# Agent attention with a cosine feed-forward: the exponentials sixteen steps later, GpSimd's row sums in wider sets

## The chip, the cores and the metric

The kernel runs on one core of one Trainium2 chip (trn2). The metric is the device time of one execution in microseconds (us); lower is better. The engines are named as the profile names them: PE is TensorE, PEld its weight loads, DVE is VectorE, ACT is ScalarE, POOL is GpSimd and SP issues the DMAs.

## What is computed

```
scale = 1 / sqrt(128)
def sm(a, b):
    s = scale * (a @ b.transpose(0, 2, 1))
    e = exp(s - s.max(-1))
    return e / (e.sum(-1) + 1e-9)
agent_v = sm(agents, k) @ v                # 4 batches, 49 agents, 12480 keys, 128 columns
x = sm(q, agents) @ agent_v                # 4 x 12480 rows, 128 columns
h = x @ w_in                               # 49920 rows, 2048 columns
out = (h * cos(h)) @ w_out                 # 49920 rows, 128 columns
```

## The kernel before

Nothing of `x` is stored. Since `x` is a product of 49 weights per query row with `agent_v`, the kernel multiplies `agent_v` into `w_in` once per batch (`project`, giving the tile `a`) and then needs, for each row, only the 49 weights. A **group** is 960 query rows (`GRP`); a batch has 13 of them. A **step** is one eighth of one half of a group: 16 steps to a group, 208 to a batch, 832 in all, and the loop at the end of the file runs over them.

In a step PE multiplies the group's turned weights `pT` with two slices of `a` (`first_product`, L1119), into a score buffer `ph` of which there are three; ACT takes the cosine (L1122); DVE forms `r = (cos - 1) * h` in one instruction (`cubic_part`, L1128); and four steps later PE multiplies `r` with `w_out` (`second_product`, L1144), whose missing linear part is added by two small products (L1140, L1141) at the end of each half group.

Everything else is done beside these steps, by a plan (`plan`, `extra`) that gives each piece of work a step number:

- *Keys*: for the next batch, 13 key groups are scored (L560), copied, and their running maximum is kept by POOL (L577 to L579); then the maximum over all is spread (`across`, `spread`) and POOL subtracts it (L604).
- *Queries*: each query group is scored (L169, L177 for some), copied, its row maximum taken (L734) and subtracted by POOL (L736, L782). Groups are gathered in **pieces** of up to seven: in each batch the eighth group up to the fourteenth, and the six behind them, which reach into the next batch. The first piece of a batch is first used at its step 128.
- *The burst*: cosine and exponential need different tables on ACT, so all exponentials of a batch are done together, at step 97 of the batch (`BURST`): the first piece of queries (L791), the keys (L607), the second piece (L791). During a burst DVE has no cosines to work on, so other work is put there (`fill`): three or four query groups of the next piece, two value groups, the test `judged`. There are four bursts, at steps 97, 305, 513 and 721. The last has no keys and no such filling.
- *Behind the burst*: POOL adds up each query row's 49 exponentials (`query_sum`, L802 to L806, a tree of additions over 24, 12, 6 and 3 columns, then three more) and, for a whole piece, adds EPS (L808); DVE takes the reciprocal of the whole piece (`query_inverse`, L814), 16 steps behind the burst for the first piece and 42 for the second. The groups of the first piece are summed at steps 1, 1, 3, 3, 9, 11 and 13 behind the burst.
- *Weights*: ten steps before a group's first step POOL multiplies its exponentials with the reciprocals (`query_weights`, L819), seven steps before it PE transposes the product (L833), ACT copies it (L838), and POOL casts it (L843) and takes what the cast lost (L844) into `pT`.
- *Values*: the 13 value groups of the next batch are multiplied with the keys' exponentials (L524) and added on DVE (L641); POOL adds the keys' exponentials (`add`, L613); then `agent_v` is folded and multiplied into `w_in` (L381).

Each engine runs its own queue in order. Where `kept_behind` or `as_traced` is used the order is as written; elsewhere a scheduler may move an instruction within its engine's queue. Around a burst PE, DVE and ACT are kept in the written order; POOL is not.

The plan of a burst, and the piece's closing addition, read:

```python
for i, n in zip((1, 1, 3, 3, 9, 11, 13), piece):
    plan(t + i, lazy_sum, n)
plan(t + (16, 42)[second], query_inverse, piece)
...
if n in closes:
    nc.gpsimd.tensor_scalar_add(rz_of[closes[n]], rz_of[closes[n]], EPS)
```

Of the kernel before, what the change touches and what calls it, by code (L numbers as in the profile page):

```python
# [9 lines left out]
F32 = mybir.dt.float32  # L10
# [8 lines left out]
P = 128  # L19
# [4 lines left out]
GT = 8  # L24
# [22 lines left out]
def agent_attention_cos_ffn(ctx, tc, qT, kT, v, vk, vk_rest, agT, w_in, w_out, outT):  # L47
# [625 lines left out]
    with ExitStack() as pools:  # L673
# [29 lines left out]
        NSTEP = NB * PER  # L703
        e_of, rz_of, closes = {}, {}, {}
        PIECES = 7

        def piece_tiles(piece):
            e = sb.tile([QT, PIECES * GT, NA], F32, name="e", bufs=3)
            rz = sb.tile([QT, PIECES * GT], F32, name="rz2", bufs=4)
            for i, k in enumerate(piece):  # L710
                e_of[k], rz_of[k] = e[:, i * GT:(i + 1) * GT], rz[:, i * GT:(i + 1) * GT]
                e_of[piece], rz_of[piece] = e[:, :len(piece) * GT], rz[:, :len(piece) * GT]
            if piece != early:
                closes[piece[-1]] = piece

# [79 lines left out]

        def query_sum(n):

            e, rz = e_of[n], rz_of[n].unsqueeze(2)
            t = sb.tile([e.shape[0], GT, 24], F32, name="tree", bufs=1)
            src, w = e, 24  # L800
            while w > 2:
                nc.gpsimd.tensor_add(t[:, :, :w], src[:, :, :w], src[:, :, w:2 * w])  # L802
                src, w = t, w // 2
            nc.gpsimd.tensor_add(rz, t[:, :, 0:1], t[:, :, 1:2])
            nc.gpsimd.tensor_add(rz, rz, t[:, :, 2:3])
            nc.gpsimd.tensor_add(rz, rz, e[:, :, 48:49])  # L806
            if n in closes:
                nc.gpsimd.tensor_scalar_add(rz_of[closes[n]], rz_of[closes[n]], EPS)  # L808

        def query_inverse(piece):  # L810
            rz = rz_of[piece]
            if piece not in closes.values():
                nc.vector.tensor_scalar_add(rz, rz, EPS)
            nc.vector.reciprocal(rz, rz)  # L814
# [43 lines left out]
        assert NG == 13  # L858
        BURST, LAST = 97, 97
        WINDOW = 7  # L860
# [96 lines left out]
        def summed(t, n):  # L957
            for x in [x for x in sums if x[1] == t][:n]:
                sums.remove(x)
                (vector_sum if x[2] else query_sum)(x[0])  # L960

        def in_parts(f, *args):
            if f is query:
                yield from query_parts(*args)
            else:
                yield f(*args)

        def lazy_sum(n):
            with kept_behind([nc.gpsimd.engine]):
                query_sum(n)  # L970

        def burst(t, todo, by_vector=False):
            (short if by_vector else windows).add(t)
            second = 0
            for f, *args in todo:
                plan(t, f, *args)
                if f is query_exp:
                    piece, = args
                    assert t + 4 < piece[0] * STEP - 10
                    if second and 16:  # L980
                        for i, n in enumerate(piece):
                            plan(t + 16 + 2 * i, lazy_sum, n)
                    elif by_vector:
                        sums.extend((n, t, True) for n in piece)
                    else:
                        for i, n in zip((1, 1, 3, 3, 9, 11, 13), piece):
                            plan(t + i, lazy_sum, n)
                    plan(t + (16, 42)[second], query_inverse, piece)
                    second = 1
# [68 lines left out]
        for b in range(1, NB):  # L1058
# [20 lines left out]
            for g in range(1, NL):  # L1079
                plan(at + 44 + 3 * g, ab[b].add, g)  # L1080
            plan(at + 44 + 3 * NL, ab[b].total)
            t, end = at + 9, o + PER - 26
# [263 lines left out]
```

## Time and profile before

| | |
|---|---|
| runs, median (lowest to highest) | 1094.3 us (1091.17 to 1095.49), 3 runs |
| profiled execution, its own time | 1090.91 us |
| its span, first to last instruction | 1089.1 us |
| busy: PE, DVE, ACT, POOL | 1038.1, 1013.8, 950.8, 564.8 us |
| granted TensorE clock, mean | 0.987 |
| DMA | 108.45 MB, mean 100 GB/s |

Times in the profile are counted from the first instruction. A row of a timeline gives start, length, engine, line, operation, the tiles written and read with their shapes, and how many alike followed each other; in brackets stands how long the engine had been idle and what ended that.

### The profile page before, as it was taken

The page shows a single profiled execution, that of the slowest core. Times are in us where ns is not written, and L with a number is a line of the kernel's source. Part 1 is how long each engine was busy: PE and PEld are TensorE (multiplying, and loading weights), DVE is VectorE, ACT ScalarE, POOL GpSimd, SP SyncE. Part 2 cuts the span into 40 slices and gives each one's busy share as a digit, 9 for nine tenths or more (in the row PEclk, how much of TensorE's full clock was granted, in tenths as well). Part 3 has the DMA queues.
Part 4 walks back from the last instruction along what each step waited for, and adds up shares of the span by engine and source line. Part 5 has one row for each costly group of instructions (what it writes and reads, how often), then busy time and mean ns, then how long its engine had stood idle before and what let it go on. Part 6 is the DMA issues. An engine that isn't in the chain of part 4 may idle for free.

```text
span 1089.1 us, 27572 instructions
## 1 busy us (share of the span) xinstructions
PE 1038.1 (95%) x11325; PEld 804.2 (74%) x11325; DVE 1013.8 (93%) x1098; ACT 950.8 (87%) x1191; POOL 564.8 (52%) x870
## 2 busy tenths in 40 slices
PE   6989999889999999989999999988999999989997
PEld 2867877777878887767787888767777777767775
DVE  6879989989999999989999999988999999999997
ACT  3669888979889998888989999897989999999996
POOL 2434876785533775777533566668462322253220
PEclk9899999999999999999999999999999999999999
DMA  9933555512202334441200334442100000000001
GB/s 349 351 94 116 157 182 190 207 39 96 80 20 76 112 117 155 137 163 59 100 38 29 123 96 159 131 149 77 61 19 38 18 37 19 37 19 37 19 37 40
DMA packets 32551, 108.45 MB, mean 100 GB/s; under 512 B 3616, under 2 KB 4896, under 8 KB 32416
## 3 DMA queue, kind: packets, MB, share of 16 engines
q1 hardware_dynamic: 32416, 106.59, 29.0%
q8 instruction: 91, 1.49, 0.6%
q14 instruction: 44, 0.36, 0.1%
HBM read 81.02 MB, written 25.56 MB: 98 GB/s over the span
## 4 chain that ended last, share of the span: by engine, by line
PE 60%; DVE 18%; POOL 12%; ACT 4%; issue 4%; DMA 1%; SPq 0%; POOLq 0%; ACTq 0%; DVEq 0%
PE ph L1119 24%; PE one L1144 22%; DVE r L1128 16%; POOL tree L802 5%; PE one L560 2%; PE one L524 2%; POOL s L604 2%; ACT c L1122 2%; PE one L169 2%; PE one L1140 1%; PE one L833 1%; PE one L1141 1%; POOL pT L844 1%; PE one L381 1%; POOL e L736 1%
## 5 line engine op out<-in xcount | busy, mean ns | idle before, releaser
L1128 DVE SCALAR_TENSOR_TENSOR r<-c,ph 128x960 fp32r<-128x960 f32 x832 | 908.8, 1149 | 37.4 <-ACT c L1122 34.8
L1122 ACT ACTIVATE c<-ph 128x960 f32<-128x960 f32 x832 | 788.9, 980 | 95.1 <-PE ph L1119 71.2
L1119 PE MATMUL ph<-pT,a 113*128 113x480 f32 x1664 | 533.0, 401 | 20.4 <-DVE r L1128 14.8
L1144 PE MATMUL one<-r,w 128*128 128x480 f32 x1664 | 503.2, 389 | 0.4 <-DVE r L1128 0.4
L1119 PEld LDWEIGHTS ph<-pT,a 113*128 113x128 f32 x1664 | 290.4, 190 | 132.8 <-DVE r L1128 67.7
L1144 PEld LDWEIGHTS one<-r,w 128*128 128x128 f32 x1664 | 308.6, 190 | 50.4 <-DVE r L1128 1.4
L819 POOL TENSOR_TENSOR p<-e,rz 126x392 f32<-126x392 f32 (+1 forms) x52 | 44.2, 851 | 188.5 <-PE one L833 181.4
L844 POOL TENSOR_TENSOR pT<-p,pT 49x480 fp32r<-49x480 f32 x104 | 127.1, 1222 | 7.9
L843 POOL CAST pT<-p 49x480 fp32r<-49x480 f32 x104 | 60.7, 584 | 56.0 <-ACT p L838 51.9
L736 POOL TENSOR_TENSOR e<-e,mx 126x392 f32<-126x392 f32 x43 | 36.1, 844 | 63.5 <-DVE mx L734 63.1
L802 POOL TENSOR_TENSOR tree<-tree 126x96 f32<-126x96 f32 (+1 forms) x141 | 43.6, 309 | 10.6
L1151 ACT COPY osb<-one 128x480 f32<-128x480 f32 x80 | 44.7, 559 | 2.3 <-PE one L1144 2.2
L604 POOL TENSOR_TENSOR s<-s,mxb 128x392 f32<-128x392 f32 (+1 forms) x39 | 34.3, 916 | 17.9 <-DVE mxb L600 17.9
L577 POOL TENSOR_TENSOR over<-s,run 128x392 f32<-128x392 f32 x27 | 28.0, 1037 | 26.9 <-ACT s L564 26.7
L524 PEld LDWEIGHTS one<-s,vt 128*32 128x32 f32 (+2 forms) x2160 | 30.5, 113 | 13.8 <-issue 10.1
L560 PEld LDWEIGHTS one<-ag,xt 128*32 128x32 f32 x2340 | 28.4, 110 | 16.2 <-issue 10.7
L1140 PE MATMUL one<-pT,b 113*128 113x480 f32 x104 | 39.9, 383 | 0.0
L1141 PE MATMUL one<-pT,b 113*128 113x480 f32 x104 | 39.6, 381 | 0.0
L524 PE MATMUL one<-s,vt 128*32 128x49 f32 (+2 forms) x2160 | 35.5, 211 | 2.3 <-ACT e L791 0.8
L578 POOL TENSOR_SCALAR over<-over 128x392 f32<-128x392 f32 x30 | 35.6, 1188 | 2.6
L560 PE MATMUL one<-ag,xt 128*32 128x49 f32 x2340 | 34.0, 209 | 2.6 <-DVE s L564 1.9
L802 POOL TENSOR_TENSOR tree<-e 126x192 f32<-126x192 f32 (+1 forms) x47 | 29.0, 616 | 14.0 <-ACT e L791 9.1
(156 smaller groups left out, 754.0 us busy)
## 6 DMA issues: line engine op xcount, KB each, us to landing
outT<-osb SPq DMA_DIRECT2D x51, 480.0 KB, 2.7
xt<-kT SPq DMA_DIRECT2D x42, 512.0 KB, 3.8
vt<-vk SPq DMA_DIRECT2D x36, 512.0 KB, 4.5
xt<-qT SPq DMA_DIRECT2D x35, 480.0 KB, 3.7
xt<-qT SPq DMA_DIRECT2D x16, 483.0 KB, 4.0
c<-kT SPq DMA_DIRECT2D x6, 512.0 KB, 5.6
c<-vk SPq DMA_DIRECT2D x6, 512.0 KB, 6.0
xt<-vk SPq DMA_DIRECT2D x6, 512.0 KB, 6.3
```

The source lines that it names most:

```text
L524: mm = nc.tensor.matmul(po[rows], vt[:, x, rows], e, start=(first and x == 0), stop=(last and x + 1 == len(es)))
L560: mm = nc.tensor.matmul(ps[j * QS:(j + 1) * QS, t], xt[:, t * w + j * QS:t * w + (j + 1) * QS], ag[:, self.b, :], start=True, stop=True)
L604: nc.gpsimd.tensor_sub(s, s, self.mxb.unsqueeze(1).to_broadcast(list(s.shape)))
L802: nc.gpsimd.tensor_add(t[:, :, :w], src[:, :, :w], src[:, :, w:2 * w])
L843: nc.gpsimd.tensor_copy(pT[own, c], p[own])
L844: nc.gpsimd.tensor_sub(pT[other, c], p[own], pT[own, c].bitcast(F32))
L1119: nc.tensor.matmul(ph[:, j, :CH], ai[:, f], pTs[q % 3][:, c], start=True, stop=True)
L1122: nc.scalar.activation(cos, h, AF.Sin, bias=HALF_PI, scale=1.0)
L1128: nc.vector.scalar_tensor_tensor(r, cos, 1.0, h, op0=ALU.subtract, op1=ALU.mult)
L1140: nc.tensor.matmul(po, b1[k], pTs[q % 3][:, c], start=False, stop=False)
L1141: nc.tensor.matmul(po, b2[k], pTs[q % 3][:, c], start=False, stop=False)
L1144: nc.tensor.matmul(po, w1[:, f, :], r[:, j, :], start=(f == 0), stop=(f == NF - 1))
```

## The change

Three things are changed.

- `BURST` is 113 instead of 97: the bursts of the first three batches come sixteen steps later (steps 113, 321 and 529). With it the scoring of keys and queries is spread up to the later step, and values, the remaining queries and POOL's additions for the keys begin later (these additions are planned 28 steps behind the burst instead of 44, so they stay where they were). The last burst stays at step 721 (`LAST`).
- POOL's sums are done for several groups in one set of instructions (`query_sums`, `added_up`): all but the last three groups of a piece, then the last three; for the first piece 1 and 3 steps behind the burst, for the second 13 and 17. EPS is added per set (L807).
- The first piece's reciprocal is in two parts, 4 and 9 steps behind the burst, one for each set. The second piece's stays whole, 42 steps behind.

```diff
--- before.py
+++ after.py
@@ -701,8 +701,10 @@
         PER = NG * STEP
         NQ = NB * NG
         NSTEP = NB * PER
-        e_of, rz_of, closes = {}, {}, {}
+        e_of, rz_of = {}, {}
         PIECES = 7
+
+        pieces_in_two = set()
 
         def piece_tiles(piece):
             e = sb.tile([QT, PIECES * GT, NA], F32, name="e", bufs=3)
@@ -710,8 +712,6 @@
             for i, k in enumerate(piece):
                 e_of[k], rz_of[k] = e[:, i * GT:(i + 1) * GT], rz[:, i * GT:(i + 1) * GT]
                 e_of[piece], rz_of[piece] = e[:, :len(piece) * GT], rz[:, :len(piece) * GT]
-            if piece != early:
-                closes[piece[-1]] = piece
 
         def query_parts(n, piece, wide=False, by_vector=False):
             b, g = n // NG, n % NG
@@ -793,10 +793,10 @@
         def vector_sum(n):
             nc.vector.reduce_sum(rz_of[n], e_of[n], axis=AX.X)
 
-        def query_sum(n):
-
-            e, rz = e_of[n], rz_of[n].unsqueeze(2)
-            t = sb.tile([e.shape[0], GT, 24], F32, name="tree", bufs=1)
+        def added_up(e, rz):
+
+            rz = rz.unsqueeze(2)
+            t = sb.tile([P, 4 * GT, 24], F32, name="tree", bufs=1)[:e.shape[0], :e.shape[1]]
             src, w = e, 24
             while w > 2:
                 nc.gpsimd.tensor_add(t[:, :, :w], src[:, :, :w], src[:, :, w:2 * w])
@@ -804,12 +804,21 @@
             nc.gpsimd.tensor_add(rz, t[:, :, 0:1], t[:, :, 1:2])
             nc.gpsimd.tensor_add(rz, rz, t[:, :, 2:3])
             nc.gpsimd.tensor_add(rz, rz, e[:, :, 48:49])
-            if n in closes:
-                nc.gpsimd.tensor_scalar_add(rz_of[closes[n]], rz_of[closes[n]], EPS)
-
-        def query_inverse(piece):
+            nc.gpsimd.tensor_scalar_add(rz, rz, EPS)
+
+        def query_sum(n):
+            added_up(e_of[n], rz_of[n])
+
+        def query_sums(piece, lo, hi):
+            part = slice(lo * GT, hi * GT)
+            with kept_behind([nc.gpsimd.engine]):
+                added_up(e_of[piece][:, part], rz_of[piece][:, part])
+
+        def query_inverse(piece, lo=0, hi=PIECES):
             rz = rz_of[piece]
-            if piece not in closes.values():
+            if piece in pieces_in_two:
+                rz = rz[:, lo * GT:hi * GT]
+            if piece == early:
                 nc.vector.tensor_scalar_add(rz, rz, EPS)
             nc.vector.reciprocal(rz, rz)
 
@@ -856,7 +865,7 @@
 
 
         assert NG == 13
-        BURST, LAST = 97, 97
+        BURST, LAST = 113, 97
         WINDOW = 7
         SHORT = 6
         windows, short = set(), set()
@@ -957,17 +966,13 @@
         def summed(t, n):
             for x in [x for x in sums if x[1] == t][:n]:
                 sums.remove(x)
-                (vector_sum if x[2] else query_sum)(x[0])
+                vector_sum(x[0])
 
         def in_parts(f, *args):
             if f is query:
                 yield from query_parts(*args)
             else:
                 yield f(*args)
-
-        def lazy_sum(n):
-            with kept_behind([nc.gpsimd.engine]):
-                query_sum(n)
 
         def burst(t, todo, by_vector=False):
             (short if by_vector else windows).add(t)
@@ -977,15 +982,18 @@
                 if f is query_exp:
                     piece, = args
                     assert t + 4 < piece[0] * STEP - 10
-                    if second and 16:
-                        for i, n in enumerate(piece):
-                            plan(t + 16 + 2 * i, lazy_sum, n)
-                    elif by_vector:
-                        sums.extend((n, t, True) for n in piece)
+                    if by_vector:
+                        sums.extend((n, t) for n in piece)
                     else:
-                        for i, n in zip((1, 1, 3, 3, 9, 11, 13), piece):
-                            plan(t + i, lazy_sum, n)
-                    plan(t + (16, 42)[second], query_inverse, piece)
+                        n = len(piece)
+                        plan(t + (1, 13)[second], query_sums, piece, 0, n - 3)
+                        plan(t + (3, 17)[second], query_sums, piece, n - 3, n)
+                    if by_vector or second:
+                        plan(t + (16, 42)[second], query_inverse, piece)
+                    else:
+                        pieces_in_two.add(piece)
+                        plan(t + 4, query_inverse, piece, 0, n - 3)
+                        plan(t + 9, query_inverse, piece, n - 3, n)
                     second = 1
 
         def scored(piece, *how):
@@ -1077,8 +1085,8 @@
             fill(at, fresh, vs, judged(at))
             fresh = [x[:3] for x in fresh]
             for g in range(1, NL):
-                plan(at + 44 + 3 * g, ab[b].add, g)
-            plan(at + 44 + 3 * NL, ab[b].total)
+                plan(at + 28 + 3 * g, ab[b].add, g)
+            plan(at + 28 + 3 * NL, ab[b].total)
             t, end = at + 9, o + PER - 26
             todo = mixed(vs, fresh)
             for i, x in enumerate(todo):
```

What this moves is seen at three places. The first is DVE's queue behind the first burst: the end of the test that fills the burst (L401, L402), then the main instructions, with `rz` the sums of a piece; before:

```order
L401 TENSOR_REDUCE t<-big 113x1
L402 TENSOR_SCALAR fits<-t 113x1
L1128 SCALAR_TENSOR_TENSOR r<-c,ph 128x960 x12
L641 TENSOR_TENSOR av<-av,one 128x49
L1128 SCALAR_TENSOR_TENSOR r<-c,ph 128x960 x4
L814 RECIPROCAL rz_1440<-rz_1440 126x56
```

and with the change:

```order
L401 TENSOR_REDUCE t<-big 113x1
L402 TENSOR_SCALAR fits<-t 113x1
L1136 SCALAR_TENSOR_TENSOR r<-c,ph 128x960 x3
L823 RECIPROCAL rz_1449<-rz_1449 126x32
L1136 SCALAR_TENSOR_TENSOR r<-c,ph 128x960 x6
L823 RECIPROCAL rz_1449<-rz_1449 126x24
```

The reciprocal of seven groups stood behind sixteen main instructions; that of four now stands behind three, and that of three behind nine.

The second is POOL's queue at the same burst: the end of the fourth group's sum, three subtractions for the filling (L736), then the cast and difference for the group that is used next, and the fifth sum; before:

```order
L806 TENSOR_TENSOR rz_1440<-rz_1440,e 126x8
L736 TENSOR_TENSOR e<-e,mx_3118 126x392
L736 TENSOR_TENSOR e<-e,mx_3121 126x392
L736 TENSOR_TENSOR e<-e,mx_3125 126x392
L843 CAST pT_99<-p 49x480 x2
L844 TENSOR_TENSOR pT_99<-p,pT_99 49x480 x2
L802 TENSOR_TENSOR tree<-e 126x192
```

and with the change, from the end of the second set on:

```order
L807 TENSOR_SCALAR rz_1449<-rz_1449 126x24
L736 TENSOR_TENSOR e<-e,mx_3277 126x392
L736 TENSOR_TENSOR e<-e,mx_3280 126x392
L736 TENSOR_TENSOR e<-e,mx_3284 126x392
L828 TENSOR_TENSOR p_104<-e,rz_1449 126x2x4x49
L828 TENSOR_TENSOR p_105<-e,rz_1449 126x2x4x49
L828 TENSOR_TENSOR p_104<-e,rz_1449 126x2x4x49
L852 CAST pT_100<-p 49x480 x2
```

All seven sums are ahead of the subtractions now, and between these and the cast stand the products of the piece's first three groups, of which the first is needed for this very cast.

The third is PE's queue at that place, nine steps behind the burst, with what each instruction waits for; before, the transposes of the group that is used next:

```order
L1119 MATMUL ph<-pT_98,a_92 128x480 [waits DVE_49]
L1119 MATMUL ph<-pT_98,a_92 128x480
L833 MATMUL one<-ident,p_105 113x126 [waits Activation_49]
L833 MATMUL one<-ident,p_105 113x126 x3
L1144 MATMUL one<-r,w_78 128x480 x2
```

and with the change:

```order
L1127 MATMUL ph<-pT_99,a_92 128x480 [waits DVE_49]
L1127 MATMUL ph<-pT_99,a_92 128x480
L842 MATMUL one<-ident,p_104 113x126 [waits Activation_49,Pool_49]
L842 MATMUL one<-ident,p_104 113x126 x3
L1152 MATMUL one<-r,w_78 128x480 x2
```

The transposes stand at the same place behind the burst, but wait for POOL, since their group is now the first of the piece whose exponentials the burst has just made.

## Rows read from the trace of the kernel before

**Rows 1.** The page, part 1: busy time of the engines.

```profile
PE 1038.1 (95%) x11325; PEld 804.2 (74%) x11325; DVE 1013.8 (93%) x1098; ACT 950.8 (87%) x1191; POOL 564.8 (52%) x870
```

**Rows 2.** Waits of the whole span: us in total, times, longest.

```profile
DVE rz L814 <- POOL rz L808: 6.8, 3, 2.3
...
PEld one L833 <- POOL p L819: 2.1, 3, 0.7
```

**Rows 3.** Stretches, L1128 on DVE: length, busy (started), clock, DMA share, GB/s.

```profile
112.70:198.40 85.70, 70.92 (x64) 1.00 0.54 167
249.60:322.70 73.10, 70.22 (x65) 1.00 0.19 66
341.10:435.10 94.00, 87.63 (x81) 1.00 0.40 128
...
853.00:939.20 86.20, 86.03 (x81) 1.00 0.07 29
```

**Rows 4.** Timeline of DVE behind the first burst.

```profile
211.78 10.86 DVE L1128 SCALAR_TENSOR_TENSOR r<-c,ph 128x960 fp32r<-128x960 f32 x10
...
225.06 4.34 DVE L1128 SCALAR_TENSOR_TENSOR r<-c,ph 128x960 fp32r<-128x960 f32 x4
231.66 0.50 DVE L814 RECIPROCAL rz<-rz 126x56 f32<-126x56 f32 x1 [2.26 <-POOL rz L808]
232.08 4.28 DVE L1128 SCALAR_TENSOR_TENSOR r<-c,ph 128x960 fp32r<-128x960 f32 x4
...
242.87 2.26 DVE L1128 SCALAR_TENSOR_TENSOR r<-c,ph 128x960 fp32r<-128x960 f32 x2 [0.71 <-ACT c L1122]
```

**Rows 5.** Timeline of PE in the same stretch.

```profile
225.25 0.60 PE L1119 MATMUL ph<-pT,a 113*128 113x480 f32 x2
...
233.23 0.69 PE L1119 MATMUL ph<-pT,a 113*128 113x480 f32 x2 [2.64 <-DVE r L1128]
...
236.46 1.00 PE L1119 MATMUL ph<-pT,a 113*128 113x480 f32 x2
```

**Rows 6.** Stretches of 2 us: PE, PEld, DVE, ACT, POOL busy, clock, DMA, GB/s.

```profile
236.00:238.00 2.00, 2.00 (x6) 1.65 (x5) 1.93 (x3) 1.37 (x2) 1.61 (x6) 0.50 0.00 0
```

**Rows 7.** Groups by line and shape: POOL's sums; busy us, mean ns, idle before.

```profile
L802 POOL TENSOR_TENSOR tree<-e 126x192 f32<-126x192 f32 x44 | 26.6, 604 | 9.8 <-ACT e L791 9.1
L802 POOL TENSOR_TENSOR tree<-tree 126x96 f32<-126x96 f32 x44 | 17.1, 388 | 3.2
...
L802 POOL TENSOR_TENSOR tree<-tree 126x24 f32<-126x24 f32 x44 | 10.3, 234 | 3.5
...
L806 POOL TENSOR_TENSOR rz<-rz,e 126x8 f32<-126x8 f32 x44 | 9.0, 205 | 3.4
```

**Rows 8.** Timeline of all engines in the first burst.

```profile
200.56 2.49 ACT L791 ACTIVATE e<-e 126x2744 f32<-126x2744 f32 x1
...
209.26 1.64 POOL L782 TENSOR_TENSOR e<-e,mx 126x392 f32<-126x392 f32 x2
...
217.88 0.59 PE L833 MATMUL one<-ident,p 126*113 126x126 f32 x4
```

**Rows 9.** Timeline of POOL behind the first burst.

```profile
214.83 2.45 POOL L736 TENSOR_TENSOR e<-e,mx 126x392 f32<-126x392 f32 x3
```

**Rows 10.** Stretches, L560 (keys scored, 64 a group) on PE; columns as rows 3.

```profile
112.70:198.40 85.70, 7.72 (x524) 1.00 0.54 167
...
341.10:435.10 94.00, 10.49 (x716) 1.00 0.40 128
```

**Rows 11.** Stretches, L169 (queries scored, 64 a group) on PE.

```profile
112.70:198.40 85.70, 10.79 (x768) 1.00 0.54 167
...
341.10:435.10 94.00, 2.70 (x192) 1.00 0.40 128
```

**Rows 12.** Stretches, L524 (values, 64 a group) on PE.

```profile
249.60:322.70 73.10, 7.69 (x528) 1.00 0.19 66
```

**Rows 13.** Line L729, its form on DVE: count, shortest, median and longest in ns.

```profile
L729 DVE COPY e<-one x11: 559/566/567, 200.6 to 719.2; 126x392 f32<-126x392 f32 x11
```

## The prediction

> **What bounds the kernel now.** I read the busy times of the page first: VectorE (DVE) and TensorE (PE) are both above 90% of the span [rows 1]. A busy PE need not be PE at its peak, so I looked for the stretch in which DVE does nothing else and never waits: in the last batch, between the third and the fourth burst, 81 of the main instructions of DVE (L1128, one per step, called a cubic here) start in 86.2 us (the last of [rows 3]), 1.064 us each, and DVE is busy for 86.03 us of it. That is the floor: 832 steps by 1.064 us are 885 us. All that a change can win lies in the stretches that run slower than that.
>
> There are three kinds. Before a burst the steps also carry the scoring of keys and queries: 1.339 us a step in batch 1 (85.7 us for 64) and 1.160 us in batch 2 (94.0 us for 81). After a burst they carry the values: 1.125 us (73.1 us for 65) [rows 3]. The third kind is the burst itself and what follows it within 45 us. In the list of waits two lines belong there, each with exactly three events, one for each main burst: DVE's reciprocal waits for GpSimd's (POOL's) sums for 6.8 us, 2.3 us at most, and PE's transposes wait for POOL's product for 2.1 us [rows 2].
>
> **What a late sum costs now.** In DVE's timeline behind the first burst the cubics run almost without a gap from 211.78 until the reciprocal of the whole first piece (126x56, seven groups) is next; it starts 2.26 us late, released by the last instruction of POOL's sums [rows 4]. The direct loss is not all. From 225.06 to 242.87 DVE does twelve cubics: four before the reciprocal, four right behind it, four in the rows left out. At 1.064 us they are 12.8 us of the 17.8. One query group is scored in that stretch; at the 0.55 us that such a group costs (worked out below) 4.5 us remain as the price of the late sum. PE shows where the rest goes. With DVE stopped no score buffer comes free, so PE idles 2.64 us [rows 5]; soon after, the granted clock is 0.50 [rows 6], the 1.2 GHz level, and a pair of matmuls there needs 1.00 us instead of 0.60 [rows 5]. So: 2.26 us of wait and 2.2 us of slow restart, three times.
>
> **The change, part by part.**
> *The sums.* A group's eight additions run on ever narrower tiles; 192, 96, 24 and 8 elements take 604, 388, 234 and 205 ns [rows 7], so some 180 ns an instruction and 2.25 ns an element. The set of four groups (768, 384, 192, 96 and three of 32 elements) is then 1900 + 1036 + 604 + 388 + 3 x 258 = 4.7 us and half a microsecond of issue between them; the set of three, from 576 down, is 4.1 us with its EPS, and again half of issue. Seven groups need 9.9 us instead of 18.
>
> *Where the first reciprocal stands.* The first exponential ends at 203.05 [rows 8]. The set of four ends near 208.3, the first addition of the next set goes ahead of its EPS in the new order, so the sum is complete near 210.3. The reciprocal of these four groups stands behind three cubics that begin at 211.78, at 215.0: 4.7 us of margin. That of the other three stands six cubics later, at 221.8, against a second set that ends near 215. Both waits go. A second reciprocal costs DVE about 0.15 us more in all.
>
> *What is late next.* The burst now comes 15 steps ahead of the first step of its own piece, so the chain exponential, sums, reciprocal, product, transposes, copy, cast and difference must close within that. POOL: two subtractions of 1.64 us [rows 8] and the rest of the second set to 215.0, three subtractions of 2.45 us [rows 9] to 217.5, the product of the piece's first group to 218.4. PE did the transposes at this place of its queue at 217.88 [rows 8]; now they wait for that product, 0.5 us, and the matmuls of the next steps stand behind them in PE's queue. DVE has no slack there, so I charge it: 0.5 us in two bursts (the third has one subtraction less). The same kind of wait at the place sixteen steps later [rows 2] goes, and was counted in the 4.5. Then the copy, one more product that POOL does first, two casts and two differences: near 223.9. The step that needs them issues its first product at 225.25 [rows 5]. Margin 1.3 us, no cost.
>
> So the late sum gives back 4.5 - 0.15 = 4.35 us three times, less twice 0.5: **12 us**. Bounds: only the wait itself (2.26 x 3 = 6.8 us, less 1.5 us of PE waits), and the whole excess with nothing for the query (5.0 x 3 = 15 us). I take the value near the upper end because the same stretch shows the clock and the recovery in its own rows.
>
> *The sixteen steps that change sides.* In batch 1 the 64 steps hold 524/64 = 8.2 key groups [rows 10] and 768/64 = 12 query groups [rows 11]: 20.2 groups, 0.315 a step, and 85.7 - 64 x 1.064 = 17.6 us over the floor, 0.87 us a group. In batch 2 11.2 + 3 = 14.2 groups on 81 steps are 0.175 a step and 0.55 us a group. Behind the burst 528/64 = 8.25 value groups [rows 12] on 65 steps are 0.127 a step and 0.48 us a group. A group costs more the closer it stands to the next. Batch 1 puts the same groups on 80 steps, 0.252 a step, by the line between the rows 0.73 us: 2.8 us won (bounds: nothing, if the price of a group is fixed, and 6.5 us at batch 2's price). Batches 2 and 3 spread about 18 groups over 112 instead of 96 steps: 0.7 us each. The values and the remaining queries, about 13 groups, close up from 106 to 90 steps: 0.4 us lost, three times. Net **3 us**.
>
> *The rest.* The last burst stays at its step, and its reciprocal did not wait; its two sets end before the places of the new reciprocals. The keys' own additions on POOL start at the same step as before. SP's loads move with the steps that use them; DMA is at a share of 0.54 or less in these stretches [rows 3]. The opening's EPS goes from DVE to POOL, one small instruction for another. Zero for all of these.
>
> Sum: 15 us. The profiled execution took 1090.9 us (span 1089.1), so 1076; the median of the runs is 3.4 us higher, and against it I predict **1079 us**.
>
> **A rule against the change.** DVE's copies during the burst take 559 to 567 ns, whether POOL adds beside them or not [rows 13]. The Trainium skill (SBUF — State Buffer, "Who interferes with whom") says that DVE and GpSimd share one pair of ports as an exclusive lock for a whole instruction, and that a copy may take it; an addition four times as long would then stop a copy four times as long. By the rows nothing is stopped even now, and the sum stays; by that rule it would be the third rival.
>
> **Rivals.**
> 1. *The wait only moves* (0.13): POOL's chain to the first group's transposed weights is 2 to 3 us longer than I added up, PE waits at the transposes or at the first product and its clock falls as now. For it: the margins are 0 and 1.3 us, and additions of 768 elements are extrapolated from 192. Against it: the four sizes lie on one line. It gives back only the 3 us of spreading and little else: 1088 to 1093 us.
> 2. *The chain ends far too late, slower* (0.05): if an element of a wide addition costs double, the two sets end 5.6 us later, and so does the product that PE's transposes wait for. PE stands 6.1 us instead of 0.5, DVE most of that, and the restart costs its 2.2 us again: 7.7 us a burst where 4.5 are lost now. Less the 3 us of spreading that is some 7 us over the median, 1097 to 1102 us. It decides from 3.3 us of wait at the transposes on, where wait and restart together eat the 4.5 us and the burst's share of the spreading. Against it: the price per element of the four sizes in the rows doesn't rise.
> 3. *Long additions stop DVE* (0.02): the additions of 1.9, 1.0, 1.5 and 0.8 us of a burst's first two sets each stop one DVE instruction for their whole length, 5.2 us a burst, and eat what is won: about 1095 us.
> 4. *The clock falls anyway* (0.02): its fall belongs to the burst and not to PE's stop. Against it: the slice at half clock lies 35 us behind the start of the burst's first exponential and right behind PE's 2.64 us [rows 5, 6, 8]. Then the waits alone are won, 6.8 us, and 3 by spreading: 1085 us, still faster.
>
> **How the numbers follow.** My case has 0.78. Its own range is 1094.3 - 23 (the upper bounds, 15 and 8) to 1094.3 - 5 (the direct wait, less the PE waits): 1072 to 1089. With the better part of rival 1 the range is 1072 to 1090. Half a per cent, 5.5 us, is about what a measurement of this kernel can tell from no change: faster means below 1088.8. Faster 0.80 (my case without its upper end, rival 4 and the better part of rival 1), same 0.15 (rivals 1 and 3 and that end), slower 0.05 (rival 2).
>
> **What would show it.** Right: no wait of DVE's reciprocal for POOL in the list; twelve cubics behind each main burst in 13 to 14 us; a granted clock of 1.00 from the burst to the values; PE's transposes with two short waits for POOL's product; the slice around the fourth burst unchanged; batch 1 before its burst at about 1.25 us a step. Wrong: PE idle before the transposes or before the first product fifteen steps behind the burst, a clock of 0.50 there, or an addition of 768 elements well over 2 us.

## The result, and the profile after

| | before | changed |
|---|---|---|
| runs, median (lowest to highest) | 1093.4 us (1091.2 to 1095.5), 4 runs | 1082.1 us (1080.2 to 1082.8), 4 runs |
| profiled execution, span | 1090.9, 1089.1 us | 1082.8, 1081.0 us |
| steps: first main instruction of DVE to the end of its last | 1017.8 us | 1005.3 us |
| granted clock, mean | 0.987 | 0.991 |

The ratio is 0.989 (95% interval 0.987 to 0.992): 11.3 us faster by the medians. The forecast was 1079.0 in a range of 1072 to 1090; the time is inside, 3 us over the forecast.

The changed kernel's page, part 1, answers [rows 1]. POOL works 33 us less for the same sums; DVE and PE hardly change:

```profile
PE 1033.9 (96%) x11325; PEld 802.6 (74%) x11325; DVE 1012.9 (94%) x1099; ACT 949.5 (88%) x1191; POOL 532.1 (49%) x670
```

Its waits answer [rows 2] (us in total, times, longest). DVE's reciprocal still waits three times for POOL, but these three lie in the opening, before 70 us; in the main bursts there is none. PE's transposes wait once in the opening and once in each of the first two main bursts:

```profile
PE one L842 <- POOL p L828: 1.1, 3, 0.5
DVE rz L823 <- POOL rz L807: 1.8, 3, 0.7
```

DVE's timeline behind the changed kernel's first burst answers [rows 4]. Both reciprocals stand directly behind main instructions, with no wait in brackets:

```profile
232.25 3.49 DVE L1136 SCALAR_TENSOR_TENSOR r<-c,ph 128x960 fp32r<-128x960 f32 x3
235.66 0.35 DVE L823 RECIPROCAL rz<-rz 126x32 f32<-126x32 f32 x1
235.92 6.44 DVE L1136 SCALAR_TENSOR_TENSOR r<-c,ph 128x960 fp32r<-128x960 f32 x6
242.27 0.30 DVE L823 RECIPROCAL rz<-rz 126x24 f32<-126x24 f32 x1
```

Where the time went is read by cutting the steps into lots of sixteen main instructions of DVE, from the start of one to the start of the sixteenth after it. Two lots around each main burst differ: the one that holds the burst ("burst lot") and the next ("lot behind"). The kernel before, the three pairs (stretch: length, DVE's busy time in L1128 and the instructions that touch the stretch, clock, DMA share, GB/s):

```profile
198.47:227.19 28.72, 17.42 (x17) 1.00 0.56 197
227.19:249.68 22.49, 17.66 (x18) 0.92 0.13 46
454.97:483.53 28.56, 17.46 (x16) 1.00 0.58 199
483.53:506.00 22.47, 17.62 (x17) 0.92 0.14 47
711.12:739.70 28.58, 17.50 (x17) 1.00 0.45 145
739.70:762.15 22.45, 17.58 (x18) 0.92 0.22 70
```

And the changed kernel (L1136), the same columns:

```profile
217.86:247.98 30.12, 17.46 (x17) 0.94 0.56 188
247.98:266.17 18.19, 17.44 (x17) 1.00 0.18 58
471.38:500.52 29.14, 17.47 (x16) 1.00 0.58 195
500.52:518.71 18.19, 17.43 (x17) 1.00 0.15 57
723.85:752.54 28.69, 17.43 (x16) 1.00 0.45 145
752.54:770.36 17.82, 17.42 (x17) 1.00 0.28 89
```

The lots behind give 4.3, 4.3 and 4.6 us, 13.2 in all, and their clock is 1.00 instead of 0.92. The burst lots lose 1.4, 0.6 and 0.1 us, 2.1 in all. A part of both is only that the reciprocal, which stood in the lot behind, now stands in two parts in the burst lot; the three pairs together are 11.1 us shorter. All other lots of the first three batches give 1.0 us and the rest 0.3; so the steps are 12.5 us shorter. In this execution the opening ahead of them was 4.1 us longer (first main instruction at 68.5 us instead of 64.4), and what follows the steps 0.3 us longer, which leaves the 8.1 us between the two spans.

### The profile page after: what moved, and what is told of

It is laid out like the page before. It is cut to its first block, busy times and chain, and to the rows that moved or that the text cites. A ratio compares the mean times of both kernels' runs of the same rounds, so it can differ in the third digit from the quotient of the medians.

```text
span 1081.0 us, 27376 instructions
## 1 busy us (share of the span) xinstructions
PE 1033.9 (96%) x11325; PEld 802.6 (74%) x11325; DVE 1012.9 (94%) x1099; ACT 949.5 (88%) x1191; POOL 532.1 (49%) x670
## 4 chain that ended last, share of the span: by engine, by line
PE 67%; DVE 17%; POOL 7%; ACT 5%; issue 3%; DMA 1%; SPq 0%; ACTq 0%; POOLq 0%; DVEq 0%
PE ph L1127 27%; PE one L1152 24%; DVE r L1136 15%; PE one L524 3%; ACT c L1130 3%; PE one L560 2%; POOL s L604 2%; PE one L842 2%; PE one L1148 2%; PE one L1149 2%; PE one L169 1%; POOL tree L802 1%; PE one L381 1%; DMA c<-kT 1%; PE ph L502 1%
## 5 line engine op out<-in xcount | busy, mean ns | idle before, releaser
L1136 DVE SCALAR_TENSOR_TENSOR r<-c,ph 128x960 fp32r<-128x960 f32 x832 | 908.2, 1150 | 31.3 <-ACT c L1130 28.1
L1127 PE MATMUL ph<-pT,a 113*128 113x480 f32 x1664 | 532.2, 400 | 13.1 <-DVE r L1136 7.1
L736 POOL TENSOR_TENSOR e<-e,mx 126x392 f32<-126x392 f32 x43 | 36.3, 849 | 73.9 <-DVE mx L734 73.4
L524 PEld LDWEIGHTS one<-s,vt 128*32 128x32 f32 (+2 forms) x2160 | 31.2, 114 | 13.6 <-issue 11.2
L560 PEld LDWEIGHTS one<-ag,xt 128*32 128x32 f32 x2340 | 28.2, 110 | 15.2 <-issue 11.4
L524 PE MATMUL one<-s,vt 128*32 128x49 f32 (+2 forms) x2160 | 36.1, 211 | 2.3 <-issue 1.4
L560 PE MATMUL one<-ag,xt 128*32 128x49 f32 x2340 | 33.6, 209 | 1.9 <-DVE s L564 1.9
L842 PEld LDWEIGHTS one<-ident,p 126*113 126x113 f32 (+1 forms) x208 | 28.9, 176 | 6.5 <-POOL p L828 2.1
L169 PEld LDWEIGHTS one<-ag,xt 128*32 128x32 f32 (+1 forms) x2112 | 25.1, 109 | 11.4 <-issue 8.5
```

The lines of the kernel that those rows point to most:

```text
L524: mm = nc.tensor.matmul(po[rows], vt[:, x, rows], e, start=(first and x == 0), stop=(last and x + 1 == len(es)))
L560: mm = nc.tensor.matmul(ps[j * QS:(j + 1) * QS, t], xt[:, t * w + j * QS:t * w + (j + 1) * QS], ag[:, self.b, :], start=True, stop=True)
L842: mm = nc.tensor.transpose(pt[:KR, t * P:t * P + rows], p_in[n % 2][:rows, t, :KR], ident[:rows, :rows])
L1127: nc.tensor.matmul(ph[:, j, :CH], ai[:, f], pTs[q % 3][:, c], start=True, stop=True)
L1136: nc.vector.scalar_tensor_tensor(r, cos, 1.0, h, op0=ALU.subtract, op1=ALU.mult)
```

## The experiments

The lots of the kernels below are cut in the same way. All medians are beside runs of the kernel before on the same chip, whose median was 1092.4 to 1093.1 us.

**The sets without the later burst**, and the changed kernel once more:

```diff
-        BURST, LAST = 113, 97
+        BURST, LAST = 97, 97
...
-                plan(at + 28 + 3 * g, ab[b].add, g)
-            plan(at + 28 + 3 * NL, ab[b].total)
+                plan(at + 44 + 3 * g, ab[b].add, g)
+            plan(at + 44 + 3 * NL, ab[b].total)
```

> The changed kernel with its main bursts back at step 97 of a batch: the sets and the split reciprocal alone. If the gain is the late sum (13.2 us by the three slices behind the bursts) and the sixteen steps are worth almost nothing after the burst slices' own 2.1 us are taken off, 1080 us, as fast as the changed kernel or 1 to 2 us faster, with no wait of PE's transposes for POOL. If the sixteen steps are worth the 3 us of the prediction, 1084 us and 2 to 3 us slower than the changed kernel. If the later burst is where the gain comes from, 1090 us or more.

> The changed kernel once more, for its opening. If the 4.1 us by which its opening was longer in the profile belong to the change (the opening's EPS on POOL), the first main instruction of DVE starts about 4 us later than in the kernel before here too. If they are the spread of the first loads from run to run, it starts within 1.5 us of it and the time is 1079 to 1082 us.

Measured: 1080.8 us (ratio 0.990, 0.988 to 0.991) with the burst at 97, and 1080.7 us (0.989, 0.987 to 0.991) for the changed kernel again. Its steps take 1005.1 us, as in the first profile (1005.3); with the burst at 97 they take 1004.5. The changed kernel's first main instruction starts at 66.6 us this time, 2.2 us later than in the kernel before, between the two expectations (more on the opening below). So the sets and the split reciprocal together bring the whole gain (neither was run by itself at step 97), and the sixteen steps are worth nothing; by the steps of the profiles they cost some 0.7 us. With the burst at 97 the three pairs of lots are 12.5 us shorter than in the kernel before. The first two pairs with the burst at 97, burst lot and lot behind:

```profile
200.99:229.93 28.94, 17.40 (x17) 1.00 0.57 196
229.93:248.11 18.18, 17.43 (x17) 1.00 0.17 57
453.36:482.29 28.93, 17.33 (x16) 1.00 0.58 196
482.29:500.48 18.19, 17.43 (x17) 1.00 0.17 58
```

The lots behind are those of the changed kernel. The first burst lot is 28.94 instead of 30.12: the changed kernel loses 1.2 us there, and both its profiles show where (stretches of 2 us of the first profile; PE, PEld, DVE, ACT, POOL busy, clock, DMA share, GB/s):

```profile
226.00:228.00 2.00, 1.13 (x32) 1.01 (x32) 1.70 (x5) 2.00 (x2) 1.69 (x6) 1.00 1.04 405
228.00:230.00 2.00, 1.59 (x35) 1.62 (x37) 1.46 (x3) 1.97 (x3) 1.84 (x3) 0.68 1.00 403
230.00:232.00 2.00, 2.00 (x36) 1.91 (x34) 0.13 (x2) 1.76 (x2) 1.92 (x4) 0.50 0.53 131
```

PE, busy for 1.13 of the 2 us before, falls to half clock (0.50) inside the burst, and the 64 value matmuls that DVE's copy waits for take 3.42 us. With the burst at 97 PE is as idle at that place (1.11 and 1.19 of 2 us) and keeps 1.00, and the same matmuls take 2.07 us. The later step alone does not decide it: the changed kernel's second burst (1.11 and 1.13 of 2 us) keeps 1.00, and so does the first burst of the kernel without the sets further down, also at step 113 (1.38 and 1.13 of 2 us, the same matmuls in 2.07 us). Why the clock falls in the one and not in the others stays open.

**The reciprocal alone, four steps later**, in the kernel before:

```diff
-                    plan(t + (16, 42)[second], query_inverse, piece)
+                    plan(t + (16 if by_vector else 20, 42)[second], query_inverse, piece)
```

> The kernel before with one number changed: the first piece's reciprocal of the main bursts planned 20 steps behind the burst instead of 16, the sums as they were. If DVE's wait for the sum is by itself what costs, it goes and 11 to 13 us are won: about 1081 us. If POOL's whole chain is late (the product that PE's transposes need stands in POOL's queue behind more sums and the reciprocal), the wait moves to PE's transposes, 2 us or more in each burst, the clock falls there, and 0 to 3 us are won: 1090 to 1093 us.

Measured: 1098.5 us (1.006, 1.004 to 1.008), slower by 6 us. DVE's wait is gone, and a longer one stands at PE's transposes. PE's timeline, first burst:

```profile
237.28 0.71 PE L1119 MATMUL ph<-pT,a 113*128 113x480 f32 x2 [0.46 <-DVE r L1128]
241.72 0.97 PE L833 MATMUL one<-ident,p 126*113 126x126 f32 x4 [3.74 <-POOL p L819]
...
243.30 1.00 PE L1119 MATMUL ph<-pT,a 113*128 113x480 f32 x2
```

and POOL and DVE there:

```profile
240.83 0.84 POOL L819 TENSOR_TENSOR p<-e,rz 126x392 f32<-126x392 f32 x1
```

```profile
245.34 1.16 DVE L1128 SCALAR_TENSOR_TENSOR r<-c,ph 128x960 fp32r<-128x960 f32 x1 [4.93 <-ACT c L1122]
```

The product for the transposes stands in POOL's queue behind three sums of the second piece and comes 3.7 us late; PE stops, the matmuls behind are at half clock (1.00 us a pair), DVE stops 4.93 us. The place of the wait was as expected, its price was not: the lots behind are 24.10, 24.77 and 25.11 us, 6.6 us more than in the kernel before.

**The same, with the second piece's sums six steps later:**

```diff
-                            plan(t + 16 + 2 * i, lazy_sum, n)
+                            plan(t + 22 + 2 * i, lazy_sum, n)
...
-                    plan(t + (16, 42)[second], query_inverse, piece)
+                    plan(t + (16 if by_vector else 20, 42)[second], query_inverse, piece)
```

> As the run with the reciprocal 20 steps behind the burst, and the second piece's single sums planned from 22 steps behind the burst on instead of 16, so that POOL reaches the first piece's products earlier. If wait and restart are the whole price and only the order of POOL's queue matters, 12 to 13 us are won without any wide set: about 1081 us. If the amount of POOL's work is what matters (18 us of single sums against 10 us of sets), products or casts come late further on and less than 6 us are won: 1087 us or more.

Measured: 1080.3 us (0.990, 0.988 to 0.991), the whole gain with the single sums as they were. POOL's product and PE's transposes in its first burst:

```profile
236.06 0.85 POOL L819 TENSOR_TENSOR p<-e,rz 126x392 f32<-126x392 f32 x1 [2.87 <-DVE rz L814]
...
237.99 0.60 PE L833 MATMUL one<-ident,p 126*113 126x126 f32 x4
```

and the lot behind:

```profile
228.77:247.30 18.53, 17.41 (x17) 1.00 0.16 56
```

The 0.35 us over 18.18 are the whole reciprocal, which lies in this lot; the two parts lie before it. What counts here is the order of POOL's queue against what DVE and PE need from it; the sets are one way to get it right, two plan numbers another.

**The later burst without the sets:** the groups of a set one after the other.

```diff
-                added_up(e_of[piece][:, part], rz_of[piece][:, part])
+                for i in range(lo, hi):
+                    part = slice(i * GT, (i + 1) * GT)
+                    added_up(e_of[piece][:, part], rz_of[piece][:, part])
```

> The changed kernel, but the groups of a set are added one after the other, as before (some 2.5 us a group instead of 4.7 and 4.1 us a set): the later burst without the wide sets. If POOL's shorter sums are what lets the burst stand at step 113, both sets end some 8 us later, the product that PE's transposes wait for as well, and each main burst costs 9 to 11 us more than in the changed kernel: 1105 to 1115 us. If the sums' length matters only to the reciprocal, which has 4.7 us of margin, within 3 us of the changed kernel: 1080 to 1084 us.

Measured: 1120.9 us (1.026, 1.024 to 1.029). The place is the expected one, the price above the range: the burst lots are 11.3, 12.8 and 11.8 us longer than the changed kernel's (41.43, 41.96 and 40.49 us), and the lot of the last burst is 2.7 us longer. A part of the price is not the sums themselves: each group has its own EPS here (0.23 us each), where the kernel before had one for a whole piece. PE's transposes, and the first of these lots:

```profile
244.99 1.19 PE L844 MATMUL one<-ident,p 126*113 126x126 f32 x4 [6.86 <-POOL p L830]
```

```profile
215.19:256.62 41.43, 17.69 (x17) 0.84 0.40 137
```

So with this order of POOL's queue the sets are what lets the burst stand at step 113, though standing there brings nothing. No other order was run with single sums at that step.

**Is the slow clock half of the price?** I had put 2.2 of the 4.5 us down to the restart at half clock [rows 5, 6]. In the kernel before, eleven matmuls by zeros fill PE's idle time:

```diff
+        blank = sb.tile([P, P], F32R, name="blank", bufs=1)
+        nc.vector.tensor_scalar_mul(blank, w1[:, 0, :], 0.0)
+
+        def filler():
+            for j in range(11):
+                nc.tensor.matmul(outs["ps"], blank, outs["r"][:, j % 2, :], start=False, stop=False)
...
+            if n - 20 in windows and n < 3 * PER:
+                with kept_behind([nc.tensor.engine]):
+                    filler()
+                    first_product(n)
```

> The kernel before, with eleven matmuls of 128x480 by a tile of zeros put into PE's queue in each main burst where PE idles 2.64 us during DVE's wait; the wait itself stays. If the part of the price beyond the wait, 2.2 us a burst, is the clock that falls after PE's idle time, the clock stays at 1.00 and the slice behind each burst goes from 22.47 to about 20.3 us: 1086 us. If it is the refilling of the queues between PE, ACT and DVE after any stop of DVE, the slices stay at 22.4 us: 1092 us. If the fillers delay the next steps, 1094 us or more.

Measured: 1093.2 us (1.001, 0.999 to 1.002): nothing. That is the time of the second expectation, but not for its reason. The lot behind keeps its length at a clock of 1.00 (second fence), so the clock is not what holds it. PE's timeline shows what does: PE runs ahead at full speed, and waits at the transposes instead.

```profile
233.35 2.13 PE L1135 MATMUL one<-r,blank 128*128 128x480 f32 x9
236.28 0.69 PE L1119 MATMUL ph<-pT,a 113*128 113x480 f32 x2 [0.80 <-DVE r L1128]
...
243.33 0.69 PE L833 MATMUL one<-ident,p 126*113 126x126 f32 x4 [1.49 <-POOL p L819]
```

```profile
230.25:252.85 22.60, 17.49 (x17) 1.00 0.14 46
```

The kernel before has the same late product. POOL starts it behind three sums of the second piece, and PE's transposes follow:

```profile
239.36 0.84 POOL L819 TENSOR_TENSOR p<-e,rz 126x392 f32<-126x392 f32 x1
```

```profile
240.25 0.69 PE L833 MATMUL one<-ident,p 126*113 126x126 f32 x4 [0.29 <-POOL p L819]
```

The wait is only 0.29 us there, because the slow clock had used up the time. Counted from the start of the lot behind, the transposes start at the same 13.1 us in the kernel before (240.25 less 227.19) and in the one with the reciprocal four steps later (241.72 less 228.60): POOL's queue sets that time, with or without DVE's wait. My theory of the restart fell; two late things lay over each other. The next pair takes the late product away and leaves DVE's wait.

**The product in time, the wait left; without and with the fillers:**

```diff
-                            plan(t + 16 + 2 * i, lazy_sum, n)
+                            plan(t + 22 + 2 * i, lazy_sum, n)
```

> The kernel before with only the second piece's single sums planned 22 steps behind the burst instead of 16: DVE's reciprocal keeps its place and its wait of 2.26 us, but POOL does the product for PE's transposes right behind the reciprocal instead of behind three more sums. If the price of 4 us a burst is how late that product comes, it is ahead of the transposes now and only DVE's wait is left: slices behind the bursts of 20.8 us instead of 22.47, about 1087 us. If the slow clock after PE's stop costs its 2.2 us as I worked out before the run, the slices stay at 22.4 us, 1092 us. If DVE's wait was harmless and the product alone was late, 18.6 us and 1081 us.

> As the run with the second piece's sums from 22 steps behind the burst, and the eleven matmuls by a tile of zeros in PE's idle time: the wait of 2.26 us, the product in time and the clock kept up. If the clock's fall has a price of its own once the product is not late, this one is 1 to 2.2 us a burst shorter than the run without the fillers: slices of 20.8 us where that shows 22 or more. If the clock costs nothing there, both show the same slices.

Measured: 1091.2 us (0.998, 0.997 to 0.999) and 1089.0 us (0.996, 0.995 to 0.997). The lots behind, all three, without the fillers:

```profile
228.07:249.95 21.88, 17.57 (x17) 0.92 0.12 47
483.70:505.59 21.89, 17.54 (x18) 0.92 0.13 48
739.40:761.31 21.91, 17.62 (x18) 0.92 0.21 71
```

and with them:

```profile
226.38:247.25 20.87, 17.35 (x18) 1.00 0.15 50
481.17:502.04 20.87, 17.35 (x18) 1.00 0.13 51
738.07:758.94 20.87, 17.35 (x18) 1.00 0.22 76
```

Neither 20.8 nor 22.4 was right for the first; 21.9 lies between. For the second, 20.87 is the length expected with the clock kept up. With the lots of the other kernels the price comes apart:

| DVE's wait | product | clock | lot behind, first burst |
|---|---|---|---|
| none | in time | 1.00 | 18.53 us |
| 2.29 us | in time | kept at 1.00 | 20.87 us |
| 2.23 us | in time | falls | 21.88 us |
| 2.26 us | late | falls (before) | 22.49 us |
| 2.26 us | late | kept at 1.00 | 22.60 us |
| none | late | falls | 24.10 us |

The wait costs its own length, 2.3 us; the slow clock 1.0 us where nothing else is late; the late product 0.6 us on top of both, 1.7 us on top of the wait with the clock kept up, and 5.6 us without the wait, where PE stops longest. The parts are not additive: each hides behind what the one before has already lost. The medians are 1.8 us and 4.0 us under the kernel before, where three lots give 1.7 and 4.8. The steps of the two profiles are only 0.8 and 1.8 us shorter: the lot of the last burst is 0.7 and 1.2 us longer in them, and with the fillers the third burst lot is 2.2 us longer. There the clock falls inside a burst at the old step:

```profile
720.00:722.00 2.00, 2.00 (x15) 1.70 (x14) 1.33 (x4) 1.25 (x2) 1.61 (x7) 0.50 0.84 250
```

**A mixture:** the changed kernel with its first burst at step 97, the others at 113, and the opening's EPS on DVE again.

```diff
-            at = o + BURST
+            at = o + (97 if b == 1 else BURST)
...
-            nc.gpsimd.tensor_scalar_add(rz, rz, EPS)
+            if eps:
+                nc.gpsimd.tensor_scalar_add(rz, rz, EPS)
...
-            if piece == early:
+            if piece == early or piece in first:
                 nc.vector.tensor_scalar_add(rz, rz, EPS)
```

> The changed kernel with its first burst back at step 97 (sets and split reciprocal kept), the second and third at 113, and the opening's EPS back on DVE. By the slices, batch 1 is 1.0 us shorter with its burst at 97, and batches 2 and 3 together 1.8 us shorter with theirs at 113, so the steps should take 1.0 us less than in the changed kernel; the opening's waits of ACT for POOL's cast (4.2 us) and of DVE for ACT (3.7 us) should fall to 2.5 to 3.5 and 2.1 us, 1 to 2 us: 1078 us. If the price of the opening is only the arrival of the first loads, and a burst's place is paid for in the batch behind it, 1080 to 1081 us as the others.

Measured: 1080.9 us (1076.8 to 1083.7; ratio 0.990, 0.988 to 0.992), no better than the others by its median. The steps do take 1.0 us less (1004.3 instead of 1005.3). In the opening ACT's wait for POOL's cast falls from 4.2 to 3.0 us. The changed kernel and this one, waits of the opening:

```profile
ACT p L486 <- POOL pT L853: 4.2, 1, 4.2
```

```profile
ACT p L486 <- POOL pT L854: 3.0, 1, 3.0
```

Over all profiles that wait is 3.7 to 4.2 us in the four with the opening's EPS on POOL and 2.5 to 3.5 us in the seven with it on DVE, and DVE's first main instruction starts at 65.8 to 68.5 us (mean 67.1) against 63.5 to 67.6 (mean 65.3). The start spreads by 3 to 4 us within each group, and PE's longest wait for the first keys is 7.0 to 9.2 us in both; so a cost of the moved EPS between 1 and 2 us is likely, not settled. No version beats the changed kernel by more than the runs spread.

## Why the prediction was right, and where it was not

- *The late sum, 12 us.* Right in its size: 13.05 us (three times 4.35) less the transposes' waits was forecast; the lots behind give 13.2, and the pairs of lots 12.5 with the burst at 97, where the reciprocals' move cancels out. The second step of it failed: "2.26 us of wait and 2.2 us of slow restart, three times". The restart costs 1.0 us, and 0.6 us was POOL's product for the transposes, late behind the second piece's sums: 4.0 us in the first burst with the wait, where I had 4.5. [Rows 5] end before it, and the wait in [rows 2] is short (2.1 us in three) only because the slow clock hid it. The sum came out because I took the price from DVE's whole stretch, which holds every cause; had the change moved only the reciprocal, the same reasoning would have missed a loss of 6 us.
- *What is late next.* Right: the transposes wait 0.5 and 0.2 us in two bursts, where I charged 0.5 each, and not in the third.
- *POOL's sums.* Right. The line through four sizes [rows 7] gave 1900 and 1036 ns for 768 and 384 elements, and would give 1468 for 576; the changed kernel's groups by shape:

```profile
L802 POOL TENSOR_TENSOR tree<-e 126x576 f32<-126x576 f32 x10 | 14.5, 1450 | 0.5
...
L802 POOL TENSOR_TENSOR tree<-e 126x768 f32<-126x768 f32 x3 | 5.6, 1873 | 1.4 <-ACT e L791 1.4
...
L802 POOL TENSOR_TENSOR tree<-tree 126x384 f32<-126x384 f32 x3 | 3.0, 1005 | 0.2
```

- *The sixteen steps, net 3 us.* Wrong. Batch 1 ahead of its burst lot and from the lot behind to its end, before:

```profile
64.39:198.47 134.08, 106.46 (x97) 1.00 0.48 146
249.68:341.13 91.45, 87.70 (x82) 1.00 0.16 58
```

and with the change:

```profile
68.45:217.86 149.41, 123.82 (x112) 1.00 0.44 135
266.17:341.50 75.33, 70.46 (x65) 1.00 0.18 64
```

The counts in [rows 3] need a correction. They are of instructions that touch a stretch, not of those that start in it. The last stretch holds 80 steps, not 81, so the floor is 1.077 us a step and not 1.064 (batch 2 has 80 and the stretch behind the burst 64). It hardly moves the prices of a group, 0.83, 0.55 and 0.51 us instead of 0.87, 0.55 and 0.48. Over 1.077 us a step the first stretch holds 30.7 us before (96 steps) and 28.8 now (112): 1.9 won where I had 2.8; the second 5.3 (80 steps) and 6.4 (64): 1.1 lost where I had 0.4. The other two batches, reckoned alike, win 1.2 and 1.1 where I had 0.7 each, and lose 1.2 and 0.9. Net 1.0 us, not 3, and the moved bursts' own lots take it back. Against the run with the bursts at 97, which differs by the sixteen steps alone, these stretches give under 0.5 us and the burst lots lose 1.4. The step that failed is the line through stretches of different density ("0.252 a step, by the line between the rows 0.73 us") together with "0.4 us lost, three times", whose price was a rough one for 13 groups: most of what spreading wins in front of the burst is lost behind it. The pace before the burst, 1.27 us a step (105.0 us for 83), is near the forecast 1.25, and told little.
- *Zero for the rest.* The burst lots with the sets alone are 0.1 to 0.4 us longer than before, since the reciprocals stand in them, and the opening's EPS is the likely 1 to 2 us above.
- *Rival 1* (the wait only moves) did not happen here; it is what the reciprocal alone did, and worse. *Rival 2* (the chain ends far too late) did not happen, as the wide additions cost what the line said; what such a chain would cost is shown by the single sums at step 113. *Rival 4*: behind the bursts the clock stays at 1.00 when PE does not stop, so its fall there belongs to the stop; the fall inside the first moved burst is another one.
- *The signs.* Twelve main instructions behind each burst take 13.4 to 13.8 us, as forecast, and the lot of the fourth burst is unchanged (22.3 and 22.2 us). The sign "a granted clock of 1.00 from the burst to the values" did not come in the first burst, where it fell to 0.50. The low end of its range is a slip of sum: 1094.3 less 23 is 1071, not 1072.
- *Rival 3* (long additions stop DVE): beside POOL's 1.87 us addition DVE's copies keep their length, 557/567/568 ns against [rows 13]; their line in the changed kernel:

```profile
L729 DVE COPY e<-one x11: 557/567/568, 220.0 to 731.9; 126x392 f32<-126x392 f32 x11
```

No addition, up to three times as long as before, stopped them; the one of 1.87 us runs from 222.54 to 224.41, a copy beside it from 223.40 to 223.97. The Trainium skill (SBUF — State Buffer, "Who interferes with whom") excepts from its lock a DVE instruction with at most one SBUF input that runs in none of the 2-port modes; these copies read PSUM, and the rows agree with the exception, though no row names the mode of a copy. If it applies, the prediction had read the rule too widely.

Against the median: 13.2 won, 2.1 lost in the burst lots, 1.3 won elsewhere, and 1 to 2 likely lost in the opening make 10.4 to 11.4 us; the runs say 11.3 and, the second time, 11.7.

## What to carry to other kernels

Price a stall by the whole stretch it disturbs, but before naming its parts follow the next consumers of the same queue: here one late queue showed as a wait of DVE, a slow clock of PE and a short wait of PE, and removing only the first made the kernel slower. When a wait is moved, look at who stands behind the new place; a change of two plan numbers did what seven rewritten sums did. A cost per item taken from stretches of different density was no measure of what spreading gave: 3 us by the line, 1 us or less in the runs.

## What the runs showed that I had not expected

- Filling PE's 2.64 us with matmuls by zeros kept its clock at 1.00 instead of letting it fall to 0.50, and changed nothing while another engine was late; with that one in time it gave 1.0 us a burst.
- A single stop of PE of 3.7 us at the transposes cost 5.6 us in the first burst (24.10 against 18.53); in the kernel before, DVE's wait and the late product together cost 4.0 (22.49).
- PE's clock fell inside the first burst in both profiles of the changed kernel, and not in the same burst sixteen steps earlier, where PE was as idle, nor in the first burst at the same later step without the sets. It fell in the third burst of the fillers' kernel too, at the old step.
